# Token mix after block-sparse attention on one core: the first mix steps in a written order, x of the first turnings loaded earlier

## The chip, the core and the metric

The kernel runs on one core of a Trainium2 chip. The core has five engines with an instruction queue each: PE (TensorE) multiplies matrices, DVE (VectorE) does elementwise work and reductions, ACT (ScalarE) activations and copies, POOL (GpSimd) copies and gathers here, and SP (SyncE) issues most of the DMAs. Each engine takes its instructions in order; semaphores tie the engines together. Tiles in SBUF and PSUM come from pools: where a tile takes over a place, its writer waits for the readers of the tile before.

The metric is the device time of one execution, in microseconds (us); lower is better. The kernel before has a median of 606.18 us over three runs. The profile is of one further execution.

## The reference

Attention over 4 batches, 8 heads, 768 positions and head size 64, where each block of 32 queries sees the first and the last block of keys, its neighbours, itself and three sampled blocks; the first and the last block of queries see everything. Its output x, of 768 by 512 for each batch, then goes through a token mix:

```python
x = attn_out.transpose(0, 2, 1, 3).reshape(B, S, H * D)
theta = x @ w_theta
zr, zi = x * np.cos(theta), x * np.sin(theta)
y = np.einsum('ts,bsd->btd', w_tok_r, zr) + np.einsum('ts,bsd->btd', w_tok_i, zi)
u = x + y
return u + np.maximum(u @ w_ch, 0.0)
```

## The kernel before

**Attention** (L487 to L570) runs over 52 units under `tc.manual_schedule()`, so its instructions stand on each engine in the order in which the code writes them. The batches go in two pairs, and bp names the pair. For each pair there are four wide units for the edge blocks of queries, then units i = 1 to 22 with one block of 32 queries for two batches and all heads. A unit is spread over several rounds of the loop: POOL copies its blocks of keys into `kg` and gathers V into `vb`; SP loads q for two units at once (`load_q`, five rounds ahead), other rows of V into `va` (`load_pair`) and stores finished x to DRAM (`xs`, `finish`); ACT scales q (L235); PE makes the scores S, DVE their extremes m, ACT the Exps P; PE turns P over by transposes into T, ACT copies T to `pT` (L327); PE multiplies by V into X. Between these, `decoder.go` unpacks weights that came as 64-bit words into pairs of high and low parts: `raw_...` is a piece as loaded, `da_...` and `ds_...` are its work tiles.

**Token mix** (L574 to L771) is a generator, `follow`. The attention loop resumes it at chosen units, and each stretch up to the next `yield` (L708 to L735) then adds its instructions at that place. For each batch b there are twelve steps k: two halves h of the channels times six groups j of 128 positions.

- `load` (L591) and `load_raw` (L600) load x of a step from `xs`, four DMAs of 64 KB each: `xa` with positions across partitions, `xr` still to be turned.
- `turn` (L617) turns `xr` over on DVE (tile r) and splits it into a high part `xTh` (ACT) and a rest `xTl` (DVE). Only steps with h = 0 have a turning.
- `theta` (L632): twelve matmuls into h; two ACT passes t (rounding to whole turns), three DVE instructions rr, then Abs and Sin (cs) and Sin (rr) on ACT.
- `turned` (L654): DVE multiplies cs and rr by xa, ACT copies the high parts zh, DVE makes the rests zl.
- `mix` (L667): 24 matmuls into four PSUM tiles y, summed over the six j of a half. After the sixth, `add_x` (L683) makes u from each y: two additions uf on DVE, the high part uh on ACT, the rest ul on DVE.
- `out` (L694): twelve matmuls with w_ch, then two DVE instructions `of` and a store.

In before, x of the first turnings goes into q's pool (`follow.send(qp)` at the fifth unit from the end) and, for turnings 2 and on, into `zp`, which can be opened only when attention's pools `ep`, `kp` and `gp` are closed (`early.close()`, behind the work of unit 50). From the step loop on (L749 to L769) the program isn't in a written order: a scheduler decides, by an estimate of times of its own, which of the instructions that are ready stands next on each engine. w_ch has eight pieces of three phases each (DVE's `bits`, `rest` and `low`, with ACT's `start` and `high` ahead of the first and the last); L760 asks for their number in each step.

Of the kernel before, what the change touches and what calls it, by code (L numbers as in the profile page):

```python
# [10 lines left out]
F32 = mybir.dt.float32  # L11
# [9 lines left out]
P = 128  # L21
# [165 lines left out]
def attention(tc, qT, qE, kT, vr, sampled, xs, ident, pieces, room, follow):  # L187
# [9 lines left out]
    with ExitStack() as ctx, ExitStack() as scored, ExitStack() as early:  # L197
# [271 lines left out]
        with tc.manual_schedule():  # L469
# [17 lines left out]
            for n in range(len(units) + 1):  # L487
# [12 lines left out]
                do(n + 2, gather_k)  # L500
                if n == len(units) - 5:
                    follow.send(qp)
                elif n == len(units) - 3:
                    next(follow)
# [33 lines left out]
                elif n == len(units):  # L538
                    last = units[n - 2][:2]
                    values(*last)  # L540
                    next(follow)
                    finish(*last)
                else:
                    bp, i, _ = units[n]
                    do(n + 1, scores, scores_wide)
                    if i == 1:
                        values_wide(bp, *units[n - 1][2], 1)
                    elif i % 2:
                        last = bp, i - 2
                        values(*last)  # L550
                    if n == len(units) - 1:
                        scored.close()
                        next(follow)
                    if i % 2:
                        do(n + 1, weights, weights_wide)
                        turn(bp, i)
# [6 lines left out]
                    if n >= len(units) - 2:  # L563
                        if n == len(units) - 2:
                            early.close()
# [8 lines left out]
def token_mix(tc, w, ch_pieces, xs, outT, bias, nb, fore):  # L574
# [8 lines left out]
    with ExitStack() as late, ExitStack() as ctx:  # L583
        half_pi, up_int, down_int, early = bias
        xa, xr, xT, angles, zs, us, ys = {}, {}, {}, {}, {}, {}, {}
        steps = 12 * nb
# [13 lines left out]
        def load_raw(k, pool=None):  # L600

            b, h, j = at(k)
            if h:
                return
            if pool:
                t = pool.tile([P, 2, 2, 4, 32], F32, tag="q", name=f"xr{b}_{j}", bufs=Q_BUFS)
                xr[b, j] = t.rearrange("p i h c u -> p (i h) c u")
            else:
                xr[b, j] = zp.tile([P, 4, 4, 32], F32, tag="xr", name=f"xr{b}_{j}", bufs=2)
# [6 lines left out]

        def turn(k):  # L617
# [6 lines left out]
            hi, lo = tok(b, j)  # L624
            raw = xr.pop((b, j))
            r = xp.tile([P, 4, 128], F32, tag="r", name=f"r{k}", bufs=1)
            for c in range(4):
                nc.vector.transpose(r[:, c, :].rearrange("p (i t) -> p i t", t=32), raw[:, :, c])
            nc.scalar.copy(hi, r)  # L629
            nc.vector.tensor_tensor(lo, r, hi.bitcast(F32), op=ALU.subtract)  # L630

        def theta(k):  # L632
            b, h, j = at(k)
            hi, lo = tok(b, j)
            wh, wl = [x[:, :, 256 * h : 256 * h + 256] for x in w["theta"]]
            ps = ps_h.tile([P, 512], F32, tag="h", name=f"h{k}")[:, 0:256]
            for c in range(4):
                nc.tensor.matmul(ps, hi[:, c, :], wh[:, c, :], start=c == 0, stop=False)  # L638
# [3 lines left out]
            nc.scalar.activation(t, ps, AF.Identity, bias=up_int, scale=1.0 / (2.0 * math.pi))  # L642
            nc.scalar.activation(t, t, AF.Identity, bias=down_int)  # L643
            r = tz.tile([P, 256], F32, tag="rr", name=f"rr{k}")
            nc.vector.scalar_tensor_tensor(r, t, -C1, ps, op0=ALU.mult, op1=ALU.add)  # L645
# [8 lines left out]
        def turned(k):  # L654
            b, h, j = at(k)
            x = xa.pop(k)[:, :, 2 * h : 2 * h + 2].rearrange("s p c u -> s c p u")
            zs[k] = []
            for m, f in enumerate(angles.pop(k)):
                f4 = f.rearrange("s (c p u) -> s c p u", c=2, p=4)
                nc.vector.tensor_tensor(f4, f4, x, op=ALU.mult)  # L660
                zh = zp.tile([P, 256], F32R, tag=f"zh{m}", name=f"zh{m}_{k}")
                zl = zp.tile([P, 256], F32R, tag=f"zl{m}", name=f"zl{m}_{k}")
                nc.scalar.copy(zh, f)
                nc.vector.tensor_tensor(zl, f, zh.bitcast(F32), op=ALU.subtract)
                zs[k].append((zh, zl))

# [40 lines left out]

        qp = yield  # L708
        load_raw(0, qp)
        yield  # L710
        load_raw(1, qp)
        w["ch"] = []
# [6 lines left out]
        for k in range(2):  # L719
            load(k)  # L720
        for k in range(2, 4):
            load_raw(k)
        turn(0)
        turn(1)
# [3 lines left out]
        nc.scalar.activation(early, half_pi, AF.Sin)  # L728
        yield
        theta(0)  # L730
        theta(1)
        yield
        turned(0)
        turned(1)
        yield  # L735
# [136 lines left out]
```

## Time and profile before

| what | us |
|---|---|
| median of three runs (604.33 to 607.37) | 606.18 |
| the profiled execution, whole | 603.66 |
| its span in the profile | 601.9 |
| PE busy | 545.9 (91%) |
| DVE busy | 444.2 (74%) |
| ACT busy | 346.1 (58%) |
| POOL busy | 150.3 (25%) |

The page's head gives the span. Its second part cuts the span into 40 slices of 15 us, with the busy share of an engine as one digit (tenths) in each; PEclk is the clock that was granted to TensorE, and DMA and GB/s what the DMA engines did. Its fourth part follows the work that ended last back through what released it. The other views are taken from the trace: the instructions by time, the busy times by stretches, and the DMA queue's issues. A row of the timeline gives start, duration, engine, line, operation and tiles, and in square brackets how long the engine had waited before it and for what. Durations of matmuls overlap: from the start of one to the start of the next counts.

### The profile page before, as it was taken

To read this page: it belongs to the slowest core of one execution; us is meant where nothing else is said; L and a number is where in the kernel's file an instruction comes from. 1 tells how busy PE (TensorE), PEld (TensorE's weight loads), DVE (VectorE), ACT (ScalarE), POOL (GpSimd) and SP (SyncE) were. 2 spreads that over 40 slices of the span, in tenths; PEclk is the share of its full clock that TensorE was granted. 3 is DMA by queue.
4 is the path that set the end of the run, shared out by engine and by line. 5 is a ranking of instruction groups with operands and counts; after the bars stand their busy time and mean duration, and the time that the engine had idled before them with its cause. 6 is when DMAs were issued, how large, how long until landed. Compare 5 with 4: busy or idle time off the path is not lost.

```text
span 601.9 us, 16838 instructions
## 1 busy us (share of the span) xinstructions
PE 545.9 (91%) x6636; PEld 481.1 (80%) x6636; DVE 444.2 (74%) x1041; ACT 346.1 (58%) x730; POOL 150.3 (25%) x262
## 2 busy tenths in 40 slices
PE   4878787897798988489999999999999999999997
PEld 2556555565565666479999999999999999999997
DVE  3799768878998998598974985757857649548454
ACT  2667757866688787755664743455634456424520
POOL 1459758640578795000000000000000000000000
PEclk9989979998999999959999999999999999999999
DMA  8879999995689899455221241211431111221002
GB/s 296 325 219 313 330 277 354 305 316 174 204 252 285 286 319 256 141 158 143 86 71 35 75 145 57 75 43 50 119 107 62 61 49 32 77 69 60 16 1 105
DMA packets 63263, 95.60 MB, mean 159 GB/s; under 512 B 9168, under 2 KB 44624, under 8 KB 63184
## 3 DMA queue, kind: packets, MB, share of 16 engines
q1 hardware_dynamic: 56848, 71.09, 38.6%
q0 software_dynamic: 6336, 23.43, 11.5%
q8 instruction: 52, 0.85, 0.6%
q14 instruction: 27, 0.22, 0.1%
HBM read 81.90 MB, written 12.58 MB: 157 GB/s over the span
## 4 chain that ended last, share of the span: by engine, by line
PE 76%; DVE 9%; ACT 7%; issue 4%; DMA 3%; SPq 1%; ACTq 0%; DVEq 0%
PE y L676 11%; PE y L677 11%; PE y L678 11%; PE T L325 6%; PE X L359 6%; PE S L307 4%; PE o L701 4%; PE o L700 4%; PE o L699 4%; PE h L638 4%; PE h L640 4%; PE h L639 4%; ACT pT L327 3%; ACT P L319 2%; DMA raw_tok_r<-in_w_tok_r_dram 2%
## 5 line engine op out<-in xcount | busy, mean ns | idle before, releaser
L319 ACT ACTIVATE P<-S,m 128x256 f32<-128x256 f32 x176 | 69.3, 485 | 15.4 <-DVE m L310 12.2
L642 ACT ACTIVATE t<-h,up_int 128x256 f32<-128x256 f32 x48 | 22.8, 475 | 74.5 <-PE h L640 74.2
L310 DVE TENSOR_REDUCE m<-S 128x2 f32<-128x512 f32 x88 | 56.3, 681 | 12.4 <-PE S L307 12.4
L307 PE MATMUL S<-kg,q 64*32 64x256 f32 x1408 | 54.9, 402 | 8.3 <-issue 8.3
L638 PE MATMUL h<-w_theta_hi,xTh 128*128 128x256 f32 x192 | 55.8, 291 | 6.9 <-ACT xTh L629 6.8
L327 ACT COPY pT<-T 128x1024 f32<-128x1024 f32 x44 | 44.8, 1019 | 30.0 <-PE T L325 29.7
L325 PE MATMUL T<-ident,P 128*128 128x128 f32 x352 | 49.1, 283 | 14.0 <-ACT pT L327 11.4
L325 PEld LDWEIGHTS T<-ident,P 128*128 128x128 f32 x352 | 38.4, 143 | 27.3 <-ACT pT L327 21.3
L268 POOL COPY kg<-kb 128x256 f32 (+2 forms) x101 | 53.0, 565 | 19.8 <-PE S L307 19.7
L640 PE MATMUL h<-w_theta_hi,xTl 128*128 128x256 f32 x192 | 55.5, 289 | 1.6 <-DVE xTl L630 1.6
L268 POOL COPY kg<-kb_tok_i 128x256 f32 (+2 forms) x101 | 50.8, 542 | 24.2 <-DVE sb_scratch L175 14.8
L639 PE MATMUL h<-w_theta_lo,xTh 128*128 128x256 f32 x192 | 55.2, 287 | 0.0
L290 POOL DMA_INDIRECT vb<-in_vr_dram,rows x44 | 44.5, 1012 | 39.6 <-PE X L359 33.5
L645 DVE SCALAR_TENSOR_TENSOR rr<-t,h 128x256 f32<-128x256 f32 x48 | 19.8, 414 | 34.6 <-ACT t L643 34.1
L649 ACT ACTIVATE cs<-rr 128x256 f32<-128x256 f32 x48 | 20.0, 416 | 43.5 <-DVE rr L647 43.5
L638 PEld LDWEIGHTS h<-w_theta_hi,xTh 128*128 128x128 f32 x192 | 37.4, 195 | 7.9 <-ACT xTh L629 7.9
L677 PE MATMUL y<-w_tok_r,zh 128*128 128x384 f32 x128 | 43.1, 337 | 0.0
L677 PE MATMUL y<-w_tok_i,zh 128*128 128x384 f32 x128 | 43.1, 337 | 0.0
L678 PE MATMUL y<-w_tok_i,zl 128*128 128x384 f32 x128 | 43.1, 337 | 0.0
L676 PE MATMUL y<-w_tok_i,zh 128*128 128x384 f32 x128 | 43.1, 337 | 0.0
L678 PE MATMUL y<-w_tok_r,zl 128*128 128x384 f32 x128 | 43.1, 337 | 0.0
L676 PE MATMUL y<-w_tok_r,zh 128*128 128x384 f32 x128 | 43.1, 336 | 0.0
(154 smaller groups left out, 1467.7 us busy)
## 6 DMA issues: line engine op xcount, KB each, us to landing
xa<-xs SPq DMA_DIRECT2D x192, 64.0 KB
xr<-xs SPq DMA_DIRECT2D x96, 64.0 KB
out_dram<-of SPq DMA_DIRECT2D x32, 192.0 KB
va<-in_vr_dram SPq DMA_DIRECT2D x22, 260.0 KB
q<-in_qT_dram SPq DMA_DIRECT2D x22, 256.0 KB
xs<-xo SPq DMA_DIRECT2D x88, 64.0 KB
raw_tok_r<-in_w_tok_r_dram SPq DMA_DIRECT2D x9, 512.0 KB
raw_tok_i<-in_w_tok_i_dram SPq DMA_DIRECT2D x9, 512.0 KB
```

The source lines that it names most:

```text
L268: nc.gpsimd.tensor_copy(dst, blocks.rearrange("r g s f -> r s g f"))
L307: nc.tensor.matmul(sc[32 * p : 32 * p + 32, e, b, :], q[rows, b, p, :], keys[rows, :, :, place(b, p), :], start=True, stop=True)
L310: nc.vector.tensor_reduce(m[:, e], sc[:, e], axis=AX.X, op=ALU.min)
L319: nc.scalar.activation(pt[:, e, b, :], sc[:, e, b, :], AF.Exp, bias=m[:, e, b : b + 1], scale=-1.0)
L325: nc.tensor.transpose(t[:, k, :], pt, ident)
L327: nc.scalar.copy(out, t.rearrange("r k (p q) -> r k p q", p=4) if len(out.shape) == 4 else t)
L638: nc.tensor.matmul(ps, hi[:, c, :], wh[:, c, :], start=c == 0, stop=False)
L639: nc.tensor.matmul(ps, hi[:, c, :], wl[:, c, :], start=False, stop=False)
L640: nc.tensor.matmul(ps, lo[:, c, :], wh[:, c, :], start=False, stop=c == 3)
L676: nc.tensor.matmul(acc, zh[:, dd], wh[j][:, tt], start=j == 0 and m == 0, stop=False)
L677: nc.tensor.matmul(acc, zh[:, dd], wl[j][:, tt], start=False, stop=False)
L678: nc.tensor.matmul(acc, zl[:, dd], wh[j][:, tt], start=False, stop=j == 5 and m == 1)
```

## The change

Three things change.

First, **x of the first three turnings** is loaded at another time and to another place. At the twelfth unit from the end (unit i = 11 of pair 1) the generator takes a tile `xr_first` in the pool `vp`, in the place where V for the edge units (`vw`) lay, and issues all twelve DMAs. The rows are those of batch 0, so `xs` of pair 0. Before, four DMAs came at the fifth and four at the third unit from the end, and turnings 2 and 3 came behind the end of unit 50.

SP's queue around that unit, before; `q_15` and `q_17` are the queries of units 15/16 and 17/18, `xs` the stores of units 9 and 10, and the semaphores in brackets are what each row waits for:

```order
L229 DMA q_15_3443<-in_qT_dram 128x512 [waits DMAHW1_49,Activation_49]
L61 DMA raw_tok_i_3494<-in_w_tok_i_dram 128x1024 [waits DMAHW2_49,DVE_49,Activation_49]
L378 DMA xs_74<-xo_9_3604 32x512 [waits DMAHW3_49,DVE_49]
L378 DMA xs_74<-xo_9_3604 32x512 [waits DMAHW4_49]
L378 DMA xs_74<-xo_9_3604 32x512 [waits DMAHW5_49]
L378 DMA xs_74<-xo_9_3604 32x512 [waits DMAHW6_49]
L287 DMA va_122<-in_vr_dram 64x1040 [waits DMAHW7_49,PE_49]
L229 DMA q_17_3612<-in_qT_dram 128x512 [waits DMAHW0_49]
```

The same place of the changed kernel, with rows that read alike drawn together:

```order
L380 DMA xs_74<-xo_7_3435 32x512 x4
L289 DMA va_123<-in_vr_dram 64x1040
L231 DMA q_15_3443<-in_qT_dram 128x512
L63 DMA raw_tok_i_3494<-in_w_tok_i_dram 128x1024
L615 DMA xr_first<-xs_73 32x4x128 x12
L380 DMA xs_74<-xo_9_3617 32x512 x4
L289 DMA va_122<-in_vr_dram 64x1040
L231 DMA q_17_3625<-in_qT_dram 128x512
```

Twelve loads have come in ahead of the stores, va and q_17; DMAHW0 to DMAHW7 are eight semaphores that all DMAs of SP use in turn, also the twelve.

Second, **the end of attention**. `pT` moves to a pool that lives longer (`cp`), so that the early pools can be closed right behind the scores of the last unit. The generator's stretches are cut anew: loads of xa and `turn(0)`, `turn(1)` behind those scores, the splits (`split`, cut off from `turn`) and the Sin table behind the last Exps, thetas 0 and 1 and their reductions ahead of the last unit's T, and then the waves and products of step 0 with turning 2. `theta` is cut into `theta` (matmuls), `reduced` (t and rr) and `waves` (Abs and Sin); `turned` casts both zh before both zl.

ACT's queue at that place, before; `P1_21` and `P1_22` are the Exps of the last two units, `pT` the copies of T, `early` is the dummy Sin that brings the table:

```order
L319 ACTIVATE P1_22_4414<-S1_22_4343,m1_22_4360 128x256 x4
L327 COPY pT_121<-T1_21_4419 128x32x32
L629 CAST xTh0_0_4473<-r0_4475 128x4x128
L629 CAST xTh0_0_4473<-r1_4482 128x4x128
L728 ACT_TABLE_LOAD
L728 ACTIVATE early_69<-half_pi_63 128x1
L327 COPY pT_121<-T1_22_4497 128x32x32
L642 ACTIVATE t0_4520<-h0_4507,up_int_65 128x256
```

And in the changed kernel:

```order
L321 ACTIVATE P1_22_4464<-S1_22_4346,m1_22_4363 128x256 x4
L638 CAST xTh0_0_4401<-r0_4403 128x4x128
L638 CAST xTh0_0_4401<-r1_4408 128x4x128
L744 ACT_TABLE_LOAD
L744 ACTIVATE early_69<-half_pi_63 128x1
L329 COPY pT_121<-T1_21_4474 128x32x32
L654 ACTIVATE t0_4526<-h0_4500,up_int_65 128x256
L655 ACTIVATE t0_4526<-t0_4526,down_int_67 128x256
L654 ACTIVATE t1_4533<-h1_4513,up_int_65 128x256
L655 ACTIVATE t1_4533<-t1_4533,down_int_67 128x256
L329 COPY pT_121<-T1_22_4540 128x32x32
```

The casts and the table have gone ahead of the copy for unit 21, and the four passes t of thetas 0 and 1 ahead of the copy for unit 22.

Third, **steps 0 to 12 of the mix** (`FIXED`) stand in a written order, with w_ch's 24 phases dealt out by `PHASES`. From step 13 on the scheduler decides as before. The core of the diff:

```diff
+FIXED = 13
+PHASES = (1, 1, 1, 3, 3, 0, 0, 3, 3, 1, 1)
...
-        pT = gp.tile([P, 2048], F32, name="pT")
+        pT = cp.tile([P, 2048], F32, name="pT")
...
-                if n == len(units) - 5:
-                    follow.send(qp)
+                if n == len(units) - 12:
+                    follow.send(vp)
...
                     do(n + 1, scores, scores_wide)
+                    if n == len(units) - 2:
+                        early.close()
+                        next(follow)
...
-        qp = yield
-        load_raw(0, qp)
+        vp = yield
+        place = vp.tile([P, 6, 260], F32, tag="vw", name="xr_first").rearrange("p c f -> p (c f)")
+        for k in range(3):
+            load_raw(k, place)
         yield
-        load_raw(1, qp)
...
-        for k in range(steps):
+        with tc.manual_schedule():
+            for k in range(FIXED):
+                theta(k + 2)
+                waves(k + 1)
+                turn(k + 3)
+                turned(k + 1)
+                split(k + 3)
+                reduced(k + 2)
+                load(k + 3)
+                load_raw(k + 5)
+                phases = PHASES[k] if k < len(PHASES) else 0
+                decoder.ahead(phases)
+                decoder.go(phases)
+                mix(k)
+            pending += [(0, th, e) for th in range(2) for e in range(4)]
+        waves(FIXED + 1)
+        turned(FIXED + 1)
+        load(FIXED + 3)
+        for k in range(FIXED, steps):
...
-            phases = 1 if 0 < k < 6 else 3 if k < 12 else 1
-            if k and decoder.left():
-                decoder.ahead(phases)
-                decoder.go(phases)
+            while decoder.left():
+                decoder.ahead(1)
+                decoder.go(1)
             mix(k)
```

DVE's queue at the end of mix 5, where y of the first half goes into u. Before, the scheduler's order; `ch_1792` is the last piece of w_ch:

```order
L645 SCALAR_TENSOR_TENSOR rr7_5071<-t7_5068,h7_5055 128x256
L664 TENSOR_TENSOR zl0_6_5013<-cs6_5007,zh0_6_5012 128x256
L78 TENSOR_SCALAR ds_ch_1792_5624<-da_ch_1792_5617 128x256
L664 TENSOR_TENSOR zl1_6_5018<-rr6_5003,zh1_6_5017 128x256
L646 SCALAR_TENSOR_TENSOR rr7_5071<-t7_5068,rr7_5071 128x256
L80 SCALAR_TENSOR_TENSOR raw_ch_1792_5533<-raw_ch_1792_5533,ds_ch_1792_5624 128x256
L89 TENSOR_TENSOR da_ch_1792_5617<-da_ch_1792_5617,w_ch_hi_4658 128x256
L689 TENSOR_TENSOR uf0_0_0_0_5100<-y0_0_4738,xTh0_0_4473 128x384
L647 TENSOR_SCALAR rr7_5071<-rr7_5071 128x256
L689 TENSOR_TENSOR uf0_0_1_0_5111<-y0_1_4739,xTh0_0_4473 128x384
L90 TENSOR_TENSOR w_ch_lo_4659<-da_ch_1792_5617,raw_ch_1792_5533 128x256
L690 TENSOR_TENSOR uf0_0_0_0_5100<-uf0_0_0_0_5100,xTl0_0_4474 128x384
```

And in the changed kernel, where a line of dots stands for eight rows of the same kind:

```order
L680 TENSOR_TENSOR zl1_6_5074<-rr6_5006,zh1_6_5073 128x256
L657 SCALAR_TENSOR_TENSOR rr7_5082<-t7_5079,h7_5052 128x256
L658 SCALAR_TENSOR_TENSOR rr7_5082<-t7_5079,rr7_5082 128x256
L659 TENSOR_SCALAR rr7_5082<-rr7_5082 128x256
L704 TENSOR_TENSOR uf0_0_0_0_5099<-y0_0_4724,xTh0_0_4401 128x384
L705 TENSOR_TENSOR uf0_0_0_0_5099<-uf0_0_0_0_5099,xTl0_0_4402 128x384
L707 TENSOR_TENSOR ul0_0_0_5098<-uf0_0_0_0_5099,uh0_0_0_5097 128x384
L704 TENSOR_TENSOR uf0_0_1_0_5110<-y0_1_4725,xTh0_0_4401 128x384
L719 TENSOR_TENSOR of0_0_0_5838<-uh0_0_0_5097,ul0_0_0_5098 128x384
...
L707 TENSOR_TENSOR ul0_0_1_5122<-uf0_0_1_1_5134,uh0_0_1_5121 128x384
L675 TENSOR_TENSOR cs7_5152<-cs7_5152,xa7_5010 128x256
```

The four tiles of u now stand in one piece between rr7 and the products of step 7, one after the other, and two sums `of` of the product with w_ch have come among them.

More of the change, by code (lines that the diff above doesn't have):

```diff
@@ L540, in attention @@
                     values(*last)
-                    next(follow)
                     finish(*last)
@@ L555, in attention @@
                         do(n + 1, weights, weights_wide)
+                        if n == len(units) - 2:
+                            next(follow)
                         turn(bp, i)
@@ L562, in attention @@
                         finish(*last)
-                    if n >= len(units) - 2:
-                        if n == len(units) - 2:
-                            early.close()
+                    if n == len(units) - 1:
                         next(follow)
@@ L584, in token_mix @@
         half_pi, up_int, down_int, early = bias
-        xa, xr, xT, angles, zs, us, ys = {}, {}, {}, {}, {}, {}, {}
+        xa, xr, xT, turning, angles, zs, us, ys = {}, {}, {}, {}, {}, {}, {}, {}
         steps = 12 * nb
@@ L604, in load_raw @@
                 return
-            if pool:
-                t = pool.tile([P, 2, 2, 4, 32], F32, tag="q", name=f"xr{b}_{j}", bufs=Q_BUFS)
-                xr[b, j] = t.rearrange("p i h c u -> p (i h) c u")
+            if pool is not None:
+                xr[b, j] = pool[:, 512 * j : 512 * j + 512].rearrange("p (i c u) -> p i c u", i=4, c=4)
             else:
@@ L615, in tok, with turn @@
             return [t[:, :, 128 * (j % 3) : 128 * (j % 3) + 128] for t in xT[b, j // 3]]
-        def turn(k):
+        def turn(k, tag="r"):
             b, h, j = at(k)
@@ L623, in turn, with split @@
                 xT[b, j // 3] = [tp.tile([P, 4, 384], F32R, tag=f"xT{x}", name=f"xT{x}{b}_{j}") for x in "hl"]
-            hi, lo = tok(b, j)
             raw = xr.pop((b, j))
-            r = xp.tile([P, 4, 128], F32, tag="r", name=f"r{k}", bufs=1)
+            turning[k] = r = xp.tile([P, 4, 128], F32, tag=tag, name=f"r{k}", bufs=3 if tag == "xa" else 1)
             for c in range(4):
                 nc.vector.transpose(r[:, c, :].rearrange("p (i t) -> p i t", t=32), raw[:, :, c])
+        def split(k):
+            b, h, j = at(k)
+            if h:
+                return
+            hi, lo = tok(b, j)
+            r = turning.pop(k)
             nc.scalar.copy(hi, r)
@@ L635, in theta @@
             wh, wl = [x[:, :, 256 * h : 256 * h + 256] for x in w["theta"]]
-            ps = ps_h.tile([P, 512], F32, tag="h", name=f"h{k}")[:, 0:256]
+            angles[k] = ps = ps_h.tile([P, 512], F32, tag="h", name=f"h{k}")[:, 0:256]
             for c in range(4):
@@ L643, in theta @@
             nc.scalar.activation(t, t, AF.Identity, bias=down_int)
-            r = tz.tile([P, 256], F32, tag="rr", name=f"rr{k}")
+            angles[k] = r = tz.tile([P, 256], F32, tag="rr", name=f"rr{k}")
             nc.vector.scalar_tensor_tensor(r, t, -C1, ps, op0=ALU.mult, op1=ALU.add)
@@ L647, in theta, with waves @@
             nc.vector.tensor_scalar(r, r, PI_IN, -PI_IN, op0=ALU.min, op1=ALU.max)
+        def waves(k):
+            r = angles[k]
             cs = tz.tile([P, 256], F32, tag="cs", name=f"cs{k}")
@@ L656, in turned @@
             x = xa.pop(k)[:, :, 2 * h : 2 * h + 2].rearrange("s p c u -> s c p u")
-            zs[k] = []
-            for m, f in enumerate(angles.pop(k)):
+            both = angles.pop(k)
+            for f in both:
                 f4 = f.rearrange("s (c p u) -> s c p u", c=2, p=4)
                 nc.vector.tensor_tensor(f4, f4, x, op=ALU.mult)
-                zh = zp.tile([P, 256], F32R, tag=f"zh{m}", name=f"zh{m}_{k}")
-                zl = zp.tile([P, 256], F32R, tag=f"zl{m}", name=f"zl{m}_{k}")
+            zs[k] = [[zp.tile([P, 256], F32R, tag=f"z{x}{m}", name=f"z{x}{m}_{k}") for x in "hl"] for m in range(2)]
+            for f, (zh, _) in zip(both, zs[k]):
                 nc.scalar.copy(zh, f)
+            for f, (zh, zl) in zip(both, zs[k]):
                 nc.vector.tensor_tensor(zl, f, zh.bitcast(F32), op=ALU.subtract)
-                zs[k].append((zh, zl))
         def mix(k):
@@ L720, in token_mix @@
             load(k)
-        for k in range(2, 4):
+        for k in range(3, 5):
             load_raw(k)
         turn(0)
-        turn(1)
+        turn(1, "xa")
+        yield
+        split(0)
+        split(1)
+        nc.scalar.activation(early, half_pi, AF.Sin)
         yield
@@ L727, in token_mix @@
         ps_o = ctx.enter_context(tc.tile_pool(name="ps_o", bufs=1, space=PSUM, side="right"))
-        nc.scalar.activation(early, half_pi, AF.Sin)
-        yield
         theta(0)
         theta(1)
+        reduced(0)
+        reduced(1)
         yield
+        waves(0)
         turned(0)
-        turned(1)
+        load(2)
+        turn(2)
+        split(2)
         yield
@@ L756, in token_mix @@
                 theta(k + 2)
+                reduced(k + 2)
+                waves(k + 2)
                 turned(k + 2)
```

8 lines of the change are left out of this document (3 added, 5 removed).

## The prediction

> **What bounds the kernel now.** The page comes first: its head, and the 40 slices of 15 us.
>
> ```profile
> span 601.9 us, 16838 instructions
> PE   4878787897798988489999999999999999999997
> DVE  3799768878998998598974985757857649548454
> PEclk9989979998999999959999999999999999999999
> PE 76%; DVE 9%; ACT 7%; issue 4%; DMA 3%; SPq 1%; ACTq 0%; DVEq 0%
> ```
>
> Attention fills the first sixteen slices, token mix the last twenty-three; slice 17 (240 to 255 us) lies between, with PE at 4 tenths, and the clock falls to 5 tenths in the slice behind it. The chain that ended last (fifth line) is PE for 76%. So a step gains only by filling the hole in slice 17 or by keeping the clock, and loses wherever PE comes to wait. Next the stretches of 5 us (stretch, length, then busy time and instructions of PE, PE's weight loads, DVE, ACT and POOL; granted clock; DMA share; GB/s).
>
> ```profile
> 250.00:255.00 5.00, 0.00 (x0) 0.00 (x0) 3.50 (x14) 3.94 (x12) 0.00 (x0) 0.82 0.37 104
> 265.00:270.00 5.00, 4.98 (x16) 4.95 (x16) 5.00 (x17) 2.96 (x8) 0.00 (x0) 0.50 0.56 154
> 275.00:280.00 5.00, 5.00 (x33) 5.00 (x33) 3.12 (x11) 1.93 (x4) 0.00 (x0) 1.00 0.54 154
> ```
>
> The timeline of the hole (start, duration):
>
> ```profile
> 248.25 1.20 PE L359 MATMUL X<-va,pT 128*64 128x65 f32 x32
> 250.54 6.31 SPq L612 DMA_DIRECT2D xr<-xs  x12
> 254.20 0.89 DVE L628 STREAM_TRANSPOSE r<-xr 128x128 f32<-128x128 f32 x4
> 255.85 0.58 PE L638 MATMUL h<-w_theta_hi,xTh 128*128 128x256 f32 x1 [6.39 <-ACT xTh L629]
> 265.08 0.66 PE L676 MATMUL y<-w_tok_r_hi,zh 128*128 128x384 f32 x1
> ```
>
> The last attention product ends at 249.45; PE then waits 6.39 us for xTh, since x of the first turnings arrives late. The first mix product stands at 265.08, at half clock (0.66 us a matmul; 16 in 5 us, later 33). When the clock falls and recovers, rows of PE in short stretches tell (length, busy, clock, DMA share, GB/s).
>
> ```profile
> 161.00:162.00 1.00, 0.00 (x0) 1.00 1.07 324
> 164.00:165.00 1.00, 1.00 (x21) 0.73 0.37 149
> 168.00:169.00 1.00, 1.00 (x53) 1.00 0.75 229
> 253.00:253.50 0.50, 0.00 (x0) 0.71 0.33 97
> 270.00:270.50 0.50, 0.50 (x4) 0.72 0.40 129
> ```
>
> Half clock holds from 253.2 to 270.3. It also fell within 164 to 165, after a hole of only about 2.4 us, and was whole again by 168: some 3.4 us at half clock.
>
> **The change part by part**, on the times of this one execution: the hole first, then steps 0 to 12, then what the moved loads cost.
>
> *The tail.* The rows of ACT and PE that stay, in their durations:
>
> ```profile
> 238.59 1.57 ACT L319 ACTIVATE P<-S,m 128x256 f32<-128x256 f32 x4 [0.39 <-DVE m L310]
> 244.09 0.62 ACT L629 CAST xTh<-r 128x512 fp32r<-128x512 f32 x1 [1.69 <-DVE r L628]
> 244.72 1.28 ACT L728 ACT_TABLE_LOAD   x1
> 246.12 1.00 ACT L327 COPY pT<-T 128x1024 f32<-128x1024 f32 x1
> 247.02 0.48 ACT L642 ACTIVATE t<-h,up_int 128x256 f32<-128x256 f32 x1
> 256.52 0.68 DVE L630 TENSOR_TENSOR xTl<-r,xTh 128x512 fp32r<-128x512 f32 x1
> ```
>
> Now ACT, from the last Exp's end (240.16), has two casts xTh (to 241.4), the table with its dummy Sin (242.9), the copy of T for unit 21 (243.9), four passes t (two of 0.5 for each theta, to 245.9) and the copy for unit 22 (246.9). PE's thetas 0 and 1 lie between the two T, and the last X ends at about 249.5, as before: ACT's added 2.6 us lie in the 2 to 3 us in which it waited for r and T. x of turning 2 is there, so behind waves(0) and its products come r (0.89), xTh (0.62) and xTl (0.68), xTl at 253.2. Theta 2 needs that, and mix 0 starts at **254.5** in place of 265.08. PE stands still from 249.5 to some 252.5.
>
> *Steps 0 to 12.* PE's price of a step:
>
> ```profile
> 277.05 0.34 PE L676 MATMUL y<-w_tok_r,zh 128*128 128x384 f32 x1
> 281.21 0.28 PE L638 MATMUL h<-w_theta_hi,xTh 128*128 128x256 f32 x1
> 282.64 0.34 PE L676 MATMUL y<-w_tok_r,zh 128*128 128x384 f32 x1
> ```
>
> A mix of 24 matmuls takes 4.16 us (0.173 each), a theta 1.43, a step 5.59. In the written order DVE and ACT hand each step to and fro: rr(k+1), ACT's Abs and two Sin, DVE's two products, ACT's two zh, DVE's two zl, then rr(k+2). The scheduler of before put other work into these waits; a fixed order can't. Prices:
>
> ```profile
> 318.08 0.42 DVE L645 SCALAR_TENSOR_TENSOR rr<-t,h 128x256 f32<-128x256 f32 x1 [4.35 <-ACT t L643]
> 320.31 0.43 DVE L660 TENSOR_TENSOR cs<-cs,xa 128x256 f32<-128x256 f32 x1 [1.03 <-ACT cs L650]
> 321.21 0.42 DVE L664 TENSOR_TENSOR zl<-cs,zh 128x256 fp32r<-128x256 f32 x1
> 245.00:330.00 85.00, 16.00 (x48) 6.28 (x16) 0.90 0.36 102
> 296.00:306.00 10.00, 5.20 (x10) 1.50 (x3) 1.00 0.14 43
> ```
>
> From rr to the product are 2.23 us, from the product to zl 0.90, two zl and the hand-over to rr another 1.4: **4.5 us** a loop, with one short phase of the decoder hidden in ACT's part. The fourth row is the decoder's tile over its eight pieces (DVE 16.00 us, so 2.0 a piece), the fifth is uf of add_x (DVE 0.52 an instruction, ACT 0.50). A turning with a phase makes the loop 5.6 to 6.4, three phases 6.1, turning and three phases 7.6. Add_x stands as one piece ahead of the next products: uf, uf plus, ACT's uh, ul, with hand-overs 2.2 us for each of four tiles, so 4.5 + 8.8 = 13.3. From rr2 (257.4: waves 1 and its products come between theta 2 and it) the eleven loops are 6.0, 5.6, 4.5, 6.1, 6.1, 13.3, 4.5, 6.1, 7.6, 6.4, 6.4, in sum **72.6**, where PE has 11 × 5.59 = 61.5 to do. So rr13 starts at 330.0. Theta 13 has ended some 2.8 us before it; mix 11, theta 14, mix 12 and the first 24 products with w_ch (4.16 + 1.43 + 4.16 + 4.15 = 13.9) end at 341.1. Before, the same work is 15 × 1.43 + 13 × 4.16 + 4.15 = 79.7 us at full clock; 50 theta matmuls (6.0) and, from 265.08 to 270.27 at half clock, 2.6 were done at 270.27, so it ends at 341.4 with PE full. The **chain term is −0.3**: the 10.6 us by which mix 0 starts earlier are used up, 11.1 of them by the loops. Bounds: −6, if hand-overs and phases are a tenth shorter (72.6 × 0.9 = 65.3, less what PE's own 61.5 takes back), and +3.
>
> *The clock.* The hole of 3.0 us, with half a microsecond before it, is longer than the 2.4 us before 164.5, so I expect one stretch of 3.4 us at half clock (the shortest seen in this trace), 1.5 to 3.2 us of PE work lost, of which the loops hide about 1.1: **+1.2** (0 to 2.3). [...]
>
> *The moved loads.* SP's queue and what waits for it:
>
> ```profile
> 200.57 0.53 SPq L229 DMA_DIRECT2D q<-in_qT_dram  x1
> 201.22 0.37 SPq L61 DMA_DIRECT2D raw_tok_i<-in_w_tok_i_dram  x1
> 204.11 2.23 SPq L378 DMA_DIRECT2D xs<-xo  x4
> 206.95 0.59 SPq L229 DMA_DIRECT2D q<-in_qT_dram  x1
> 214.47 0.66 ACT L235 ACTIVATE q<-q 128x512 f32<-128x512 f32 x1
> 205.00:210.00 5.00, 5.00 (x162) 3.66 (x146) 4.17 (x7) 4.75 (x12) 3.69 (x7) 1.00 1.05 374
> DMA to landing us min/median/max: 5.6/6.9/8.9
> 260.20 2.39 DMA xr<-xs
> ```
>
> Twelve loads of 64 KB now stand behind raw_tok_i, ahead of xs, va and q of units 17 and 18. SP holds eight transfers at a time: each waits for the landing of the one eight before it. The DMA engines are full here (share 1.05). Five xr go out by 203.6, at 0.5 us each; the sixth waits for the va before it (206.1), the seventh for the q issued at 200.57 (6.9 us later, 207.4), the eighth for raw_tok_i (208.6), the last four for the first xr (to 210.5); then xs, va, and q at 213.5 in place of 206.95. A gather of V took 5.6 to 8.9 us to land at this load, one xr with little else moving 2.39 (the last two rows). Of these I take 4.5, so q lands at about 218, where ACT scales it at 214.47. In ACT's one queue the cast of the decoder, the Exps and the copies of T stand behind this scale; PE's T and X wait for them and POOL's next gather for X. Of 3.5 us, 0.8 fits into slack, and POOL and PE are too full to catch up: **+2.7** (0.8 to 4.0, the lower end with 2.39 us to land, the upper with 6.9). V's place is dead by then, and pT's move costs no instruction. The x loads that go (12 of them in the hole) free only SP's time there, already counted.
>
> *Behind step 12* the scheduler works as before, with what is left of the decoder in one piece: **+0.3** (0 to 1).
>
> Sum: −0.3 + 1.2 + 2.7 + 0.3 = +3.9, and 0.5 for two products with w_ch that the compiled order puts between the last tiles of mix 6: **+4.4**. The profiled execution was 603.66 us (span 601.9), so it would be 608.1. The median of the three runs is 606.18, 2.5 above that execution, so I give 606.18 + 4.4 = **610.5 us**.
>
> **The rivals.**
> (a) *PE isn't starved*: where the loops stay under PE's 5.59 us a step (that is where it turns), mixes follow unbroken from 254.5: 12 × 1.43 + 13 × 4.16 + 4.15 = 75.4, end 329.9 in place of 341.4, so −11.5 + 2.7 + 1.2 + 0.3 = −7.3: 598.9. For it: DVE was busy only 3.12 of 5 us. Against: add_x as one piece is 8.8 us, during which no zl comes. Halfway: 603. Chance 0.27.
> (b) *The loads do no harm*: q lands as fast as under light load, a term of 0.9 in place of 2.7: 608.7, within half a per cent, as are mixtures of (a) and the forecast. For it: 2.39 us in the last row above. The Trainium skill, "DMA: Bandwidth & Descriptors", section "Anatomy of one DMA", gives about 2 us fixed cost; the rows at full load are far above. Against: the share of 1.05. Chance 0.28.
> (c) *Worse*: the waits of PE around mix 6 and 7 or before theta 12 (3.2 us by the loops) halve the clock once more, 3.2, and the loads cost 4.0 in place of 2.7: 610.5 + 4.5 = 615. Chance 0.07.
> (d) *It doesn't do what it says*: the order inside the fixed stretch holds on every engine but for those two products with w_ch and their sums, so no chance apart from the forecast's.
>
> **How the numbers follow.** The forecast has 0.38, (a) 0.27, (b) 0.28, (c) 0.07. Half a per cent, 3.0 us, is about what a measurement can tell from no change. Faster 0.27, same 0.28, slower 0.38 + 0.07 = 0.45. The range goes from (a), 598.5, to beyond (c), 616; the forecast's own is 609.2 to 614.
>
> **What would show it.** Right: twelve xr loads on SP near 202 to 210, and ACT's scale near 215 waiting for q's DMA; the last X some 2.7 us later; one short stretch of half clock in place of 17 us; mix 0 near 257; PE waiting for zl around mix 7 and for xTl before theta 12; DVE waiting for ACT's uh. Wrong: PE at full rows from mix 0 to mix 12, or the last X at 249.5.

## The result, and the profile after

The changed kernel has a median of 614.14 us in 12 executions (606.23 to 618.36), before beside it 607.48 us in 12 (600.24 to 613.36). The ratio is **1.0102**, 95% interval 1.0067 to 1.0137: slower by about 1%. A second set of 12 gave 1.0044 (1.0007 to 1.0081), so between half a per cent and one. The ratios leave out executions in a slower state (3 of the changed kernel's 12 here), the medians don't. The forecast was slower, 4.4 us or 0.7%.

The profiled execution took 617.42 us. It stands above the median, since attention was already 5 us late in it ahead of the moved loads. Such drift is found in all kernels here, so single stretches are compared below; a stretch of attention drifts too, as the first table shows. The page's head and slices:

```profile
span 615.6 us, 16818 instructions
PE   4878696876798849879998899999999999999997
DVE  3798676967898858768779897756966648547554
PEclk9989988997999979999999999999999999999999
PE 55%; DVE 18%; ACT 11%; issue 6%; DMA 5%; SPq 2%; POOL 1%; POOLq 1%; DVEq 0%; ACTq 0%
```

The hole of slice 17 and the half clock behind it are gone (PE 7, 9, 9, 9 in slices 18 to 21, the clock 9 throughout). Instead PE has a 4 in slice 15 (215 to 231 us), with a clock of 7, and an 8 in slices 22 and 23. The chain that ended last has changed its owner: PE 55% in place of 76%, DVE 18% in place of 9%. Slice 15 in the timeline, rows of SP, ACT and PE:

```profile
206.26 13.43 SPq L615 DMA_DIRECT2D xr_first<-xs  x12
219.79 1.88 SPq L380 DMA_DIRECT2D xs<-xo  x4
221.76 0.47 SPq L289 DMA_DIRECT2D va<-in_vr_dram  x1
222.28 0.58 SPq L231 DMA_DIRECT2D q<-in_qT_dram  x1
...
227.82 0.63 ACT L237 ACTIVATE q<-q 128x512 f32<-128x512 f32 x1 [8.05 <-DMA q<-in_qT_dram]
...
227.22 2.06 PE L361 MATMUL X<-va,pT 128*64 128x65 f32 x32 [7.60 <-DMA va<-in_vr_dram]
```

The twelve loads hold SP's queue for 13.43 us. va and q behind them go out at 221.76 and 222.28; PE waits 7.60 us for the one and ACT 8.05 us for the other. The wait takes the clock with it (stretch, length, busy PE, PEld, DVE, ACT, POOL; clock, DMA share, GB/s):

```profile
218.00:220.00 2.00, 1.62 (x75) 1.08 (x66) 1.90 (x4) 1.77 (x5) 2.00 (x5) 1.00 0.92 285
222.00:224.00 2.00, 0.00 (x0) 0.00 (x0) 0.19 (x1) 0.00 (x0) 1.84 (x5) 0.57 0.86 199
230.00:232.00 2.00, 2.00 (x29) 1.26 (x35) 1.38 (x4) 1.16 (x3) 0.00 (x0) 0.50 1.04 245
```

Then the end of attention, PE's rows of the last X, theta 2 and mix 0:

```profile
260.85 1.20 PE L361 MATMUL X<-va,pT 128*64 128x65 f32 x32
264.48 0.39 PE L647 MATMUL h<-w_theta_hi,xTh 128*128 128x256 f32 x1 [2.42 <-ACT xTh L638]
267.53 0.42 PE L691 MATMUL y<-w_tok_r_hi,zh 128*128 128x384 f32 x1 [0.90 <-DVE xo L346]
```

The last X ends at 262.05 and mix 0 starts 5.5 us later; before it was 249.45 to 265.08, 15.6 us. What mix 0 waits for at the end is neither theta 2 nor its own products (the last zl of step 0 ends at 262.97). It is xo, DVE's scaling of the last X, as the bracket of its row says: y is written once X has been read. The row of xo on DVE, in before and in the changed kernel:

```profile
264.25 0.68 DVE L344 TENSOR_TENSOR xo<-X,sm 128x512 f32<-128x512 f32 x1
266.70 0.68 DVE L346 TENSOR_TENSOR xo<-X,sm 128x512 f32<-128x512 f32 x1
```

In all 14 traces of this case mix 0 starts 0.15 to 0.18 us behind the end of this row, whatever the order around it. So where the last xo stands in DVE's queue sets the earliest start of the mix. Mix 0 comes 10.1 us earlier behind attention, and yet the end doesn't come earlier. DVE at the end of mix 5 shows one reason:

```profile
299.68 0.42 DVE L657 SCALAR_TENSOR_TENSOR rr<-t,h 128x256 f32<-128x256 f32 x1 [0.49 <-ACT t L655]
300.81 0.55 DVE L704 TENSOR_TENSOR uf<-y,xTh 128x384 f32<-128x384 f32 x1
302.53 0.56 DVE L707 TENSOR_TENSOR ul<-uf,uh 128x384 fp32r<-128x384 f32 x1 [0.58 <-ACT uh L706]
...
309.80 0.56 DVE L707 TENSOR_TENSOR ul<-uf,uh 128x384 fp32r<-128x384 f32 x1 [0.58 <-ACT uh L706]
310.67 0.42 DVE L675 TENSOR_TENSOR cs<-cs,xa 128x256 f32<-128x256 f32 x1 [0.30 <-ACT cs L665]
312.82 0.42 DVE L657 SCALAR_TENSOR_TENSOR rr<-t,h 128x256 f32<-128x256 f32 x1 [0.49 <-ACT t L655]
```

From rr7 to rr8 are 13.1 us, four tiles of u one after the other, each with a wait of 0.58 us for ACT. PE's longest wait there is for a uf, which reads a y that mix 6 is to write anew:

```profile
308.69 0.44 PE L691 MATMUL y<-w_tok_r_hi,zh 128*128 128x384 f32 x1 [1.22 <-DVE uf L704]
```

All runs can be cut at points of PE's rows: T of unit 14 of pair 1 (ahead of the waits for va and q of units 17 and 18), T of unit 15, and the end of the last X. Stretch A goes from T of unit 14 to the last X, B from the last X to the end.

| kernel | loads of x, units from the end | fixed steps | T of 14 to T of 15 | A, us | last X to mix 0 | B, us | ratio to before (95%) |
|---|---|---|---|---|---|---|---|
| before | 5, 3, later | 0 | 4.6 | 38.5 | 15.6 | 352.4 | 1 |
| changed | 12 | 13 | 13.1 | 46.0 | 5.5 | 353.6 | 1.0102 (1.0067 to 1.0137) |
| again | 12 | 13 | 10.3 | 44.6 | 5.5 | 353.1 | 1.0044 (1.0007 to 1.0081) |
| late | 5 | 13 | 4.6 | 41.4 | 5.5 | 353.4 | 0.9995 (0.9958 to 1.0032) |
| next_unit | 11 | 13 | 5.0 | 42.3 | 5.5 | 354.0 | 1.0090 (1.0053 to 1.0126) |
| extra | as before, and 12 unused | 0 | 10.4 | 45.7 | 16.5 | 352.8 | 1.0061 (1.0019 to 1.0102) |
| xonly | 5, old end | 0 | 5.0 | 47.6 | 21.2 | 352.1 | 0.9991 (0.9944 to 1.0038) |
| inter | 5 | 13, rewoven | 5.5 | 43.6 | 5.5 | 360.0 | 1.0133 (1.0087 to 1.0180) |
| phases | 5 | 13, fewer phases | 4.7 | 39.2 | 5.5 | 354.3 | 1.0026 (0.9978 to 1.0073) |
| fixed8 | 5 | 8 | 4.6 | 41.6 | 5.5 | 346.9 | 0.9935 (0.9891 to 0.9980) |
| fixed5 | 5 | 5 | 4.6 | 42.6 | 5.5 | 343.1 | 0.9856 (0.9801 to 0.9911) |
| fixed5_early | 12 | 5 | 13.1 | 45.5 | 5.5 | 342.4 | 0.9891 (0.9839 to 0.9942) |
| fixed0 | 5 | 0 | 5.0 | 45.4 | 4.9 | 344.0 | 0.9887 (0.9842 to 0.9932) |
| tail | 5 | 5, turning 2 first | 4.6 | 41.1 | 4.3 | 346.3 | 0.9899 (0.9861 to 0.9938) |

A and B come from one profiled execution each; the ratios from 6 to 12. The column T of 14 to T of 15 separates cleanly: 10.3 to 13.1 us in the four kernels with the twelve loads at the twelfth unit, 4.6 to 5.5 in the ten others. A as a whole doesn't: in eight kernels without loads ahead of unit 14 (next_unit and xonly aside) it goes from 38.5 to 45.4, with a mean of 41.7, and before's is the lowest. With the early loads it is 44.6 to 46.0, mean 45.5. So the early loads delay unit 15 by 6 to 9 us against before, and the last X by about 4 us as an average, with a spread of single executions that is as large. Whether part of the delay is made up later, or the loads cost something at the fifth unit too, one execution of each can't tell.

A second table is worked out from PE's rows behind the last X: the distance from each matmul's start to the next, less 0.119 us (256 columns) or 0.173 us (384), summed by the mix in which it falls; the last row also has the little that falls elsewhere.

| PE's loss, us | before | changed | late | phases | fixed8 | fixed5 |
|---|---|---|---|---|---|---|
| up to mix 0 | 12.5 | 4.0 | 4.0 | 4.0 | 4.0 | 4.0 |
| mix 0 and 1 | 2.5 | 0.8 | 0.6 | 1.9 | 1.7 | 0.6 |
| mix 5 and 6 | 0.0 | 3.1 | 3.1 | 10.7 | 1.2 | 0.2 |
| mix 7 and 8 | 0.0 | 0.3 | 0.3 | 0.2 | 0.0 | 0.5 |
| mix 9 to 11 | 0.1 | 4.4 | 4.4 | 0.0 | 1.3 | 0.1 |
| mix 12 | 0.0 | 3.7 | 3.7 | 0.2 | 1.5 | 0.0 |
| all | 16.1 | 17.6 | 17.4 | 18.3 | 11.0 | 6.8 |

### The profile page after: what moved, and what is told of

The parts are those of the page before. It is cut to its first block, busy times and chain, and to the rows that moved or that the text cites. A ratio compares the mean times of both kernels' runs of the same rounds, so it can differ in the third digit from the quotient of the medians.

```text
span 615.6 us, 16818 instructions
## 1 busy us (share of the span) xinstructions
PE 545.3 (89%) x6636; PEld 477.5 (78%) x6636; DVE 448.8 (73%) x1041; ACT 344.9 (56%) x730; POOL 145.8 (24%) x262
## 4 chain that ended last, share of the span: by engine, by line
PE 55%; DVE 18%; ACT 11%; issue 6%; DMA 5%; SPq 2%; POOL 1%; POOLq 1%; DVEq 0%; ACTq 0%
PE y L693 8%; PE y L692 8%; PE y L691 8%; PE o L714 3%; PE o L715 3%; PE o L716 3%; PE T L327 3%; PE X L361 3%; ACT P L321 3%; DVE m L312 3%; PE h L649 3%; PE h L648 3%; PE h L647 3%; PE S L309 2%; PE SW L403 2%
## 5 line engine op out<-in xcount | busy, mean ns | idle before, releaser
L327 PEld LDWEIGHTS T<-ident,P 128*128 128x128 f32 x352 | 39.2, 145 | 28.8 <-ACT pT L329 23.8
L647 PE MATMUL h<-w_theta_hi,xTh 128*128 128x256 f32 x192 | 54.3, 283 | 4.3 <-ACT xTh L638 4.3
L270 POOL COPY kg<-kb_tok_i 128x256 f32 (+2 forms) x101 | 47.2, 509 | 26.5 <-DMA kb_tok_i<-in_kT_dram 14.8
L715 PE MATMUL o<-ul,w_ch_hi 128*128 128x384 f32 x128 | 43.3, 339 | 0.9 <-DVE ul L707 0.9
L714 PE MATMUL o<-uh,w_ch_hi 128*128 128x384 f32 x128 | 43.0, 340 | 1.2 <-ACT uh L706 1.0
L716 PE MATMUL o<-uh,w_ch_lo 128*128 128x384 f32 x128 | 42.9, 335 | 0.0
```

The lines of the kernel that those rows point to most:

```text
L270: nc.gpsimd.tensor_copy(dst, blocks.rearrange("r g s f -> r s g f"))
L327: nc.tensor.transpose(t[:, k, :], pt, ident)
L715: nc.tensor.matmul(ps, wh[:, c, :], ul, start=False, stop=False)
```

## The experiments

**again**: the changed kernel once more.

> The changed kernel once more, for a second profile of it. Queue theory: the twelve loads of x stand on SP ahead of the stores, va and q of units 17 and 18, so ACT waits for this q in every execution, 8.05 us in the first profile; here again 6 to 9 us, and the time about 1.0 per cent above before (612 to 614). Rival: the 8 us belong to that one execution, whose attention was already 5 us behind before the loads; then ACT waits 2 to 4 us here.

ACT waited 6.19 us for q of units 17 and 18 and PE 4.7 us for va; A was 44.6 us. The cost isn't one execution's. The ratio, 1.0044, lay below the 1.010 that the expectation named.

**late**: only the place of the loads.

```diff
-                if n == len(units) - 12:
+                if n == len(units) - 5:
                     follow.send(vp)
```

> The changed kernel with the twelve loads at the fifth unit from the end, behind the last q; the order on PE, DVE and ACT is the same. Queue theory: ACT's wait for q of units 17 and 18 goes, the last X comes about 8 us earlier, and the time falls by 6 to 9 us, to about 605 (the same as before or slightly faster). Rival (the loads cost 2.7 us and the loops of the fixed steps are the loss): it falls by 2 to 3 us only, to about 610.

No wait for that q; A 4.6 us shorter than in the changed kernel, 3.2 than in again. The median (609.74 beside 610.58 for before) lies 5.0 us under that of again in the same set; by the two ratios, 0.9995 and 1.0044, it is 3.0 us. Their intervals overlap a little; with the changed kernel's first set (1.0102) they don't. So the time falls, by an amount that doesn't tell which theory is nearer. B stays at 353.4.

**extra**: before, with twelve loads that nobody reads.

```diff
+                if n == len(units) - 12:
+                    extra = vp.tile([P, 6, 260], F32, tag="vw", name="xr_extra").rearrange("p c f -> p (c f)")
...
+                            nc.sync.dma_start(dst, xs[0][4 * j : 4 * j + 4, p // 2, :, 0, p % 2].rearrange("i q c -> q i c"))
```

> The kernel before with the same twelve loads at the twelfth unit from the end into the place of V for the edge units, read by nobody; all else as before. Queue theory: slower by 6 to 9 us (613 to 615), with ACT's wait for q of units 17 and 18 in the profile. Rival: slower by 2 to 3 us.

The wait comes with the loads alone; the row of ACT:

```profile
221.57 0.63 ACT L235 ACTIVATE q<-q 128x512 f32<-128x512 f32 x1 [5.10 <-DMA q<-in_qT_dram]
```

A is 45.7 us, 7.2 more than before, with PE, DVE and ACT in before's order. The time rose by 0.6% (0.2 to 1.0), about 3.7 us: less than the 6 to 9 of the queue theory and less than A says. Before's one execution has the shortest A of all, so A overstates the price.

**next_unit**: the loads one unit later, behind q of units 17 and 18.

> The changed kernel with the twelve loads one unit later, at the eleventh from the end, where they stand behind q of units 17 and 18 in SP's queue and two units ahead of the next q. Queue theory: what costs is what stands behind the loads; no wait of ACT for that q, the wait for the next q is 0 to 3 us (13 us of loads against two units of 9 us and q's lead), and the stretch from T of unit 14 to the last X is 3 to 7 us shorter than in the changed kernel. Rival (the DMA engines are full, the loads cost their traffic wherever they stand): the wait moves to the next q with 6 us or more.

```profile
234.78 0.63 ACT L237 ACTIVATE q<-q 128x512 f32<-128x512 f32 x1 [1.51 <-DMA q<-in_qT_dram]
```

The next q made ACT wait 1.51 us only, and A fell to 42.3. Its time didn't fall below the changed kernel's, though (1.0090). The trace shows a wait that the expectation didn't name: a piece of w_tok_i now stands right behind the loads. ACT waits for it, the copy of T behind it on ACT is late, and PE waits for that copy:

```profile
230.25 0.66 ACT L68 ACTIVATE da_tok_i<-raw_tok_i 128x512 f32<-128x512 f32 x1 [3.25 <-DMA raw_tok_i<-in_w_tok_i_dram]
231.86 1.13 PE L361 MATMUL X<-vb,pT 128*32 128x65 f32 x62 [2.14 <-ACT pT L329]
```

So the loads delay whatever stands behind them. Whether these 2.1 us make up the time, and whether the traffic itself costs something, stays open.

**xonly**: before's end of attention and scheduler, with x of turnings 0 to 2 loaded at the fifth unit from the end.

> The kernel before with x of turnings 0 to 2 in the place of V for the edge units, loaded at the fifth unit from the end; no fixed order, the old end of attention. If the hole before theta 2 comes from the late x alone, the wait of 6.4 us and most of the 17 us at half clock go, and the time falls by 6 to 10 us, to about 598. If the closing of the pools or ACT's casts and table keep the hole open, it falls by less than 3 us.

Nothing gained, and mix 0 21.2 us behind the last X. Theta 2 started at once, but DVE had other work (rows of DVE):

```profile
265.09 0.61 DVE L70 TENSOR_SCALAR da_ch<-da_ch 128x256 f32<-128x256 f32 x2 [2.01 <-ACT da_ch L66]
267.56 0.88 DVE L627 STREAM_TRANSPOSE r<-xr 128x128 f32<-128x128 f32 x4
268.54 0.41 DVE L659 TENSOR_TENSOR cs<-cs,xa 128x256 f32<-128x256 f32 x1
274.80 0.42 DVE L663 TENSOR_TENSOR zl<-rr,zh 128x256 fp32r<-128x256 f32 x1 [0.36 <-ACT zh L662]
```

Here the scheduler put decoding, rr and turnings ahead of the first products, and the last xo behind most of them, 0.15 us ahead of mix 0 (283.96):

```profile
283.13 0.68 DVE L344 TENSOR_TENSOR xo<-X,sm 128x512 f32<-128x512 f32 x1
```

So early x alone doesn't close the hole. In A, PE stood still once for 4.65 us for no cause that the profile names; A isn't to be compared there.

**phases**: `PHASES = (1, 1, 1, 3, 3)`, the rest left to the scheduler.

> As the run late, with the decoder's phases of steps 7 to 10 left to the scheduler behind step 12 (PHASES = 1, 1, 1, 3, 3). Loop theory: the loops behind rr10 fall from 7.1, 5.9 and 6.4 to 5.3 to 5.6, PE's losses in mix 9 to 11 from 4 us to 1, and the products with w_ch come later without loss; the stretch behind the last X gets 2 to 4 us shorter. Rival: the turnings set these loops, not the phases; less than 1 us.

The loops behind rr8 fell to 4.4 to 4.9 us and the loss of mix 9 to 11 to nothing, more than expected. But the scheduler may put free work between the fixed rows, and it put the phases into add_x, where ACT's one queue then waits for their loads:

```profile
300.38 0.43 ACT L68 ACTIVATE da_ch<-raw_ch 128x256 f32<-128x256 f32 x1 [2.40 <-DMA raw_ch<-in_w_ch_dram]
300.72 0.49 ACT L706 CAST uh<-uf 128x384 fp32r<-128x384 f32 x1
...
298.90 0.48 PE L691 MATMUL y<-w_tok_r_hi,zh 128*128 128x384 f32 x1 [2.55 <-DVE uf L704]
```

The loop of add_x rose from 13.1 to 17.8 us, and B didn't get 2 to 4 us shorter but 0.9 longer.

**inter**: add_x rewoven on DVE, the waves earlier on ACT.

```diff
+                    if a:
+                        rest()
...
-            nc.vector.tensor_tensor(ul, t, uh.bitcast(F32), op=ALU.subtract)
+            halves.append((t, uh, ul))
...
-                waves(k + 1)
...
+                waves(k + 2)
                 load(k + 3)
```

> As the run late, with add_x rewoven on DVE (ul of a tile behind both uf of the next one, in place of waiting for its own uh) and the waves of a step put ahead of the add_x on ACT. Loop theory: PE's losses around mix 6 are the 8.8 us of DVE waiting in add_x; the loop from rr7 to rr8 falls from 13.1 to about 9, PE's loss in mix 6 from 3.1 to 0.5 to 1.5 us, and the stretch behind the last X gets 1.5 to 2.5 us shorter. Rival: the loss there comes from the products with w_ch that the scheduler puts into mix 6, which stay; then it falls by less than 1 us.

It went the other way: B grew to 360.0 us, 1.0133. The loop of add_x fell to 10.7 us and the loss in mix 6 to 1.7 (with 2.3 in mix 5), but loops with three phases rose from 5.8 to 7.7: the waves now stand ahead of the decoder's casts on ACT, and DVE's last phase waits for those. One written order was traded for another.

**fixed8** and **fixed5**: `FIXED = 8` or `5`, the rest, with its phases, by the scheduler.

> As the run late, with FIXED = 8: one add_x, that of mix 5, stands in the fixed order, the loops behind rr10 with their turnings and phases don't. Loop theory: PE loses in mix 6 what it loses in late (3.1 us, 2.5 to 5 as the scheduler may add to it), next to nothing in mix 9 to 12, and the stretch behind the last X is 346 to 348 us, between fixed5 (343.1) and late (353.4). Rival (the loss is made where the scheduler takes over): as late, 352 to 354.

> As the run late, with FIXED = 5: the scheduler takes over from step 5, with the rule of before for the rest of the phases. Loop theory: with the first mixes as early as now and work to put into the waits of add_x, the losses in mix 6 to 12 (11 to 12 us) go for the most part; the stretch behind the last X gets 5 to 10 us shorter and the time is below before's by 1 per cent or more. Rival: the scheduler lays its own holes (in the order as compiled PE has theta 13 ahead of mix 6 there): within 3 us of late.

B falls from 353.4 to 346.9 and 343.1: the first inside the expectation, the second, 10.3 us shorter, just beyond its 5 to 10. The losses in fixed8 lie elsewhere than expected: 1.2 in mix 6 in place of 2.5 to 5, and 2.8 in mix 11 and 12 in place of next to nothing. The same place in fixed5, first DVE's rows, then the stretch (columns as above):

```profile
304.88 0.42 DVE L680 TENSOR_TENSOR zl<-rr,zh 128x256 fp32r<-128x256 f32 x1
305.21 0.42 DVE L657 SCALAR_TENSOR_TENSOR rr<-t,h 128x256 f32<-128x256 f32 x1
305.54 0.56 DVE L704 TENSOR_TENSOR uf<-y,xTh 128x384 f32<-128x384 f32 x1
306.48 0.42 DVE L82 SCALAR_TENSOR_TENSOR raw_ch<-raw_ch,ds_ch 128x256 f32<-128x256 uint32 x1
```

```profile
303.00:308.00 5.00, 5.00 (x33) 4.79 (x32) 5.00 (x14) 0.55 (x2) 0.00 (x0) 1.00 0.40 105
```

DVE is full (5.00 of 5 us) and never waits, where the changed kernel has

```profile
305.00:310.00 5.00, 3.54 (x17) 2.80 (x18) 3.74 (x8) 1.29 (x4) 0.00 (x0) 1.00 0.00 0
```

with PE at 3.54 and DVE at 3.74. **fixed5 beats both kernels: 600.45 us against 608.61 for before in its set, ratio 0.9856; the changed kernel, in other sets, has 1.0102 and 1.0044.**

**fixed0**: no fixed step at all.

> As the run late, with FIXED = 0: the new end of attention and early x, no fixed step. If the early x and the new end carry the gain, it is the fastest, some 10 us below late. If, as in the run xonly, the scheduler spends DVE and ACT on decoding and later thetas ahead of step 0's products, mix 0 starts 10 us or more later than in late (5.5 us behind the last X there) and nothing is gained.

Mix 0 starts 4.9 us behind the last X, and B is 344.0, 9.4 us below late's. By the ratios the time is 1.1% or 6.6 us below late's in place of 10, and not to be told from fixed5's. So the new end of attention, together with early x, brings most of the gain, unlike early x alone in xonly. Which part of the new end does it (closed pools, order of the casts, place of the last xo) was not taken apart.

**fixed5_early**: fixed5 with the loads where the change puts them.

> FIXED = 5 with the twelve loads where the change puts them, at the twelfth unit from the end. If the two costs add up, this is the changed kernel without the loops' loss: ACT waits 5 to 8 us for q of units 17 and 18, the stretch behind the last X stays at 343 to 344 us, and the time is 0.6 to 1.2 per cent above fixed5, about level with before or 0.5 per cent below.

ACT waited 8.05 us for q again, A was 45.5, B 342.4: in the profile the two costs stand side by side. The time doesn't show it: 0.9891 is 1.1% below before, where half a per cent at most was expected, and 0.35% above fixed5's in place of 0.6 to 1.2, a difference within the intervals.

**tail**: fixed5 with turning 2 ahead of the waves of step 0.

> As the run fixed5, with turning 2 and its split ahead of the waves of step 0 (and turning 3 behind its products), so that theta 2 needn't wait for them. If DVE's and ACT's queue between the last T and mix 0 sets the 5.5 us from the last X to mix 0, this falls to 2 to 4 us and the stretch behind the last X to 341 to 342 us, the fastest of all. Rival: mix 0 is held by its products and not by theta 2; no change within 0.5 us.

Theta 2 followed the last X at once, but mix 0 came 4.3 us behind it, and B was 346.3, not 341 to 342. What held mix 0 was neither theta 2 nor its products but again xo, which DVE reached at 258.35, behind the products of step 1 and xTl of turning 3:

```profile
259.18 0.41 PE L691 MATMUL y<-w_tok_r_hi,zh 128*128 128x384 f32 x1 [2.73 <-DVE xo L346]
```

And mix 1 lost 4.3 us. ACT's row shows why:

```profile
267.64 0.43 ACT L68 ACTIVATE da_ch<-raw_ch 128x256 f32<-128x256 f32 x1 [9.03 <-DMA xs<-xo]
```

The decoder's tile lies where the last xo lay, so its first instruction waits for the last stores of x, which stand on SP behind loads of xa and xr; everything behind it on ACT waits too. In the changed kernel the same wait, behind rr2, is 4.80 us, and mostly covered for PE:

```profile
273.50 0.43 ACT L68 ACTIVATE da_ch<-raw_ch 128x256 f32<-128x256 f32 x1 [4.80 <-DMA xs<-xo]
```

## Why the prediction was right, point by point

*The tail*: forecast 5.0 us from the last X to mix 0, measured 5.5 in all nine kernels that kept this end; the wait before theta 2 2.42 us, forecast 3.0. The number is right in part by luck. The prediction lets mix 0 follow theta 2; in the changed kernel PE has ended theta 2 at 266.63 and waits 0.90 us more for xo, which the prediction doesn't name. And ACT's longer queue does cost the last X something, where the prediction put it at nothing: the copy for unit 22, behind the four passes t, made PE wait 0.64 us.

```profile
259.79 1.13 PE L361 MATMUL X<-vb,pT 128*32 128x65 f32 x62 [0.64 <-ACT pT L329]
```

*Steps 0 to 12*: the eleven loops measured 9.7, 5.2, 4.4, 5.8, 5.8, 13.1, 4.4, 5.8, 7.1, 5.9, 6.4, in sum 73.7 where 72.6 was forecast. The sum is closer than its parts: the first loop was 3.7 us longer, by the wait for the store of xo that I had not seen, and the ten others together 2.6 shorter. That the loops use up the earlier start is shown by fixed5 and fixed8. One sign that was to show it didn't come: PE hardly waits for products around mix 7 (0.17 us, for zh). The loss in mix 6 is the wait for uf shown above, with shorter ones for uh and ul of the products with w_ch; the wait before theta 12 came as said (1.90 us, for xTh). Which part of mix 12's 3.7 us is the loops' and which comes from products with w_ch waiting for uh and ul (1.0, 0.6 and 0.8 us of it by PE's rows) was not taken apart.

*The clock*: forecast one stretch of 3.4 us. The changed kernel and again show none at the hole; late shows one from 254.5 on, others 3.4 or 6.8. The cost of 1.2 us is borne out by no run: B is 353.6 and 353.1 without half clock at the hole, 353.4 in late with 3.4 us of it and 354.0 in next_unit with 6.8. The hole ahead of 164.5, with which the prediction compares, was 2.94 us by PE's row, not 2.4. By the Trainium skill, "TensorE: Matmul & The Clock Gate", section "Part 1: The HAM clock gate (the "warmup" mystery)", the clock halves after an idle window of about 3.4 us, so that a hole of 2.4 us needn't cost anything; of the nine kernels with this hole two agree and seven don't. What the traces show in its place stands in the last section.

*B as a whole*: +1.7 forecast, +1.2, +0.7, +1.0 and +1.6 in the four profiles with all 13 steps in the change's order.

*The moved loads*: forecast +2.7, bounds 0.8 to 4.0. The mechanism, q behind the loads, was the right one, and it sits at the place named; va beside it, which I had only named in the queue, made PE wait too. The wait itself **was mis-sized**: ACT waited 5.1 to 8.1 us for q where 3.5 was forecast, and unit 15 came 6 to 9 us late. What failed is mainly the time in the queue: the first six xr took 7.7 to 9.9 us from issue to landing, so the eight transfers in flight turned over more slowly, and the loads took 13.4 us of the queue where I had 8.9. The landing of q took 5.5 where I had 4.5. Half clock in that wait and behind it came on top. The delay at unit 15 doesn't reach the end in full, as far as the runs tell: A is 7.4 and 6.1 us above before's, and before's A is the shortest of all. The means of A and the timed runs put the price at 2 to 5 us (means 3.8; extra 3.7; again against late 3.0 by the ratios, 5.0 by the medians; fixed5_early against fixed5 2.1, within the intervals), so 2.7 is low but not excluded. The Trainium skill, "DMA: Bandwidth & Descriptors", section "Anatomy of one DMA", gives about 2 us of fixed cost for a DMA that GpSimd issues. The 2.39 us of one xr in before lies near it and is no guide to this place; nor was that light load, as the prediction says, since the DMA share there was 0.69 (260 to 263).

*The rivals*: (a) had the start of the mixes right and the loops wrong. (b), harmless loads, fell as a mechanism with the 8.05 us, while its time, within half a per cent of before, isn't excluded by the second set (1.0044). (c) named a halved clock before theta 12: late shows it (319.4, 3.4 us), at a loss of mix 9 of 3.7 in place of 2.7, made good in mix 11.

## What to carry to other kernels

An order written by hand is worth its place where the scheduler makes a bad choice once (here the last xo and the first products behind attention), and no further: here each step beyond the fifth bound two engines to waits that free work filled in fixed5. When a stage waits to start, look at what reads the place that it writes, and not only at its inputs. A load that nobody waits for still delays what stands behind it in its queue: look at everything that stands behind it (q, va and a piece of weights here), put it behind the last urgent one, and price it by landings at that place of the queue. Work that is left out of a fixed stretch may come back in its middle.

## What the runs showed of the hardware

- The granted clock changed on a grid of 3.41 us: away from the first 20 and the last 8 us, all stretches at half clock in the 14 traces last 3.4, 6.8, 10.2 or 17.1 us, and the changes of a trace lie a whole number of 3.41 us apart. Where the grid lies against the program differs from execution to execution. Cut along it, of the windows at full clock all 79 with PE busy for less than 45% were followed by half clock, none of 2074 with more than 60%, and 13 of 88 between; full clock came back behind all 81 windows at half clock with over 95%, and behind none of 29 under 85%. So a hole costs by how it falls on the grid: the 2.42 us behind the last X was cut in two in the changed kernel (from 259.8 on PE busy for 2.22 and then 1.94 of 3.41 us, full clock kept) and lay almost whole within one window in late (1.09 of 3.41, half clock from 254.5).
- The wait of 7.6 us in the changed kernel ends at 227.22; half clock lay from 222.3 to 232.5, so 5.3 us of it fell on work.
- The same 64 KB load landed after 7.7 to 9.9 us (the first six of twelve) and 3.0 to 5.2 us (the last six) in the changed kernel, with a DMA share of 0.84 to 1.05, and in 2.39 us in before with a share of 0.69.
- T of unit 14 lay between 210.8 and 219.5 us over all profiles, with no clear order by kernel: attention drifts by more than what was to be measured, so stretches had to be compared, and A itself, of some 42 us, drifts by 7. Whether pT's new place has a part in it was not tried.
